# Moving weight and input loads, and cutting output tiles into half steps, in a fused attention and bilinear FFN kernel

## The chip, the cores and the metric

The kernel runs on one core of a Trainium2 chip. A core has five engines with instruction streams of their own: TensorE (PE, with its weight loads shown as PEld), VectorE (DVE), ScalarE (ACT), GpSimd (POOL) and SyncE (SP), and sixteen DMA engines that serve all DMA queues. The metric is device time in microseconds (us) of one execution; lower is better. Loads that change the type from float32 to bfloat16 are issued here from GpSimd (queue q0 of the profile); output stores and DMA transposes are issued from SyncE (queue q1).

## The reference

There are 4 batches of 8 heads, 768 rows and 64 columns a head. Rows form 8 blocks of 96. A small 8x8 matrix per head (`sort_net`) is normalised five times over rows and columns, and mixes the blocks of k and v. Each block of q then attends to its mixed block alone. The result, turned to 3072 tokens of 512 columns, goes through a bilinear FFN.

```python
for _ in range(5):
    P = exp(P - max(P)); P = P / sum(P, -1); P = P / sum(P, -2)
k_sorted = einsum('bhij,bhjcd->bhicd', P, k_b)      # the same for v
scores = scale * matmul(q_b, k_sb^T)                # per block of 96 rows
attn = softmax(scores)
x = matmul(attn, v_sb)                              # 4*768 tokens x 512
out = ((x @ w_a) * (x @ w_b)) @ w_out               # 512 -> 1536 -> 512
```

## The kernel before

Heads are worked in pairs: four pairs a batch, sixteen in all, numbered 0 to 15; pairs 4 to 7 are batch 1, pairs 8 to 11 batch 2. A pair has three units of attention work. **M** (`M`, line 507) mixes k and v with the spread matrices `s_all` (`pair_mix`, matmuls of line 281, copied to kT and vT by ScalarE and VectorE), turns v by a DMA transpose from SyncE (`turn_v`), and prepares the next pair's q: a copy on GpSimd (`pair_q`, line 265, two buffers `qc`) and a DMA transpose (`turn_q`, line 271, tile `qTf`). **R** (`pair_scores`) makes the scores (line 301) and their exponentials on ScalarE. **O** (`pair_o`) makes the outputs (line 249), has VectorE take reciprocals and scale them (lines 253 and 255, tile `xp`), in two halves, and turns them into `xT` by a DMA transpose (line 321). The score, output and mix tiles of PSUM share two buffers (pool `psA`).

The FFN of a batch is a list of steps on TensorE. `ffn_ab(b, m, t)` makes block m (128 columns) of x@w_a and x@w_b for half t of the tokens, eight matmuls of line 336, copied by ScalarE (356) and multiplied by VectorE (357) into `hT`. The output of batch 0 is made by `ffn_out` (line 377), six tiles of twelve matmuls with w_out, each copied by ScalarE (even tiles) or VectorE (odd tiles) to `o_sb`, which has two buffers, and stored by two DMAs. Batches 1 to 3 use Strassen's products instead (`ffn_out_pair`, line 434), with sums of the quarters of w_out that VectorE makes during batch 1 (`weight_sums`); only the last token tiles of batch 3 use plain products.

The order of all five engines is that of the program, written by hand (line 533). `interleave` (line 523) puts the attention units of batch b+1 between the FFN steps of batch b: after each step it emits units until their number reaches a share of the steps done. For batch 0's second half the steps are twelve `ffn_ab` and six `ffn_out`; the parameter `outs` counts each `ffn_out` as two steps. The order of the units of a batch is M0 M1 R0 M2 R1 O0 M3 R2 O1 R3 O2 O3, with the pair's number within the batch.

GpSimd issues the loads in program order and runs ahead of TensorE as far as buffers and DMA tracking allow: in the trace each load's issue starts just after the landing of the load eight places before it. A pair's k, v and q are loaded by three DMAs (`load_pair`, line 100; six buffers of each). The FFN weights w_a and w_b are loaded in six chunks of 256 columns each (`load_ab`, line 110), w_out in three (`load_out`, line 115). GpSimd also makes parts of `s_all` (`spread`, line 157) and the q copies. Pair 8's load is issued in O of pair 6, pair 9's in O of pair 7, pair 10's and 11's in M of pairs 8 and 9.

SyncE takes its transposes and stores in program order too, so each waits for those before it.

Of the kernel before, what the change touches and what calls it, by code (L numbers as in the profile page):

```python
# [9 lines left out]
FP32 = mybir.dt.float32  # L10
BF16 = mybir.dt.bfloat16
# [11 lines left out]
def kernel(  # L23
# [11 lines left out]
    nc = tc.nc  # L35
    P = 128
    B, H, S, D = q.shape
# [3 lines left out]
    DMODEL = H * D  # L41
# [4 lines left out]
    NCH = S // P  # L46
    HP = H // 2
    NPAIR = B * HP
    KA = DMODEL // P
    KO = DFF // P  # L50
    KH = KO // 2
# [6 lines left out]
    V0 = 16  # L58
    W = NCH * D
    HW = S // 2  # L60
    WC = 256
    NBUF = 3
    PSUM = bass.MemoryType.PSUM
    ET = mybir.EngineType
# [1 line left out]
    const = ctx.enter_context(tc.tile_pool(name="const", bufs=1))  # L66
# [5 lines left out]
    outp = ctx.enter_context(tc.tile_pool(name="outp", bufs=1))  # L72
    psA = ctx.enter_context(tc.tile_pool(name="psA", bufs=2, space=PSUM))
    psF = ctx.enter_context(tc.tile_pool(name="psF", bufs=4, space=PSUM))
# [18 lines left out]
    def load_pair(g):  # L93
        base = 2 * g * S * D
        tiles = []
        for name, t in (("k2", k), ("v2", v), ("q2", q)):
            if g < HP and name == "q2":
                continue
            to = ld.tile([P, 2, W], BF16, tag=name, name=name)
            nc.gpsimd.dma_start(out=to, in_=_ap(t, base, [[W, P], [S * D, 2], [1, W]]))  # L100
            tiles.append(to)
        loaded[g] = tiles
# [3 lines left out]
    w_out_sb = const.tile([P, KO, DMODEL], BF16, name="w_out_sb")  # L106

    def load_ab(c):
        for w_ap, w_sb in ((moe_w_a, w_a_sb), (moe_w_b, w_b_sb)):
            nc.gpsimd.dma_start(  # L110
                out=w_sb[:, :, c * WC:(c + 1) * WC],
                in_=w_ap.rearrange("(kc p) n -> p kc n", p=P)[:, :, c * WC:(c + 1) * WC])

    def load_out(c):
        nc.gpsimd.dma_start(
            out=w_out_sb[:, c * 4:(c + 1) * 4, :],
            in_=moe_w_out.rearrange("(kc p) n -> p kc n", p=P)[:, c * 4:(c + 1) * 4, :])
# [12 lines left out]
    kTs = [const.tile([P, S + PAD], BF16, name=f"kT{n}") for n in range(NBUF)]  # L130
# [23 lines left out]
    p_col = const.tile([P, NB, BH], BF16, name="p_col")  # L154

    def spread(eng, src, h0, n, i0=0, ni=NB):
        eng.tensor_tensor(
            out=s_all[:, h0:h0 + n, i0:i0 + ni],
            in0=_ap(mask, 0, [[CG, P], [0, n], [0, ni], [1, CG]]),
            in1=_ap(src, i0 * BH + h0, [[NB * BH, P], [1, n], [BH, ni], [0, CG]]),  # L160
            op=ALU.mult)

    def copy(eng, out, in_):
        if eng == "act":
            nc.scalar.copy(out=out, in_=in_)  # L165
        else:
            nc.vector.tensor_copy(out=out, in_=in_)
# [92 lines left out]

    def pair_q(g):
        qc = qtp.tile([P, NCH, 2, D], BF16, tag="qc", name="qc", bufs=2)
        nc.gpsimd.tensor_copy(out=qc.rearrange("p c e d -> p e c d"),  # L265
                              in_=loaded[g][2].rearrange("p e (c d) -> p e c d", c=NCH))
        st[g, "qc"] = qc

    def turn_q(g):
        qT = qtp.tile([P, NCH, P], BF16, tag="qTf", name="qTf", bufs=3)  # L270
        nc.sync.dma_start_transpose(out=qT, in_=st[g, "qc"].rearrange("p c e d -> p (c e d)"))
        st[g, "qT"] = qT

    def pair_mix(g, what, engines):
        src2 = loaded[g][0 if what == "k" else 1]
        to = (kTs if what == "k" else vTs)[g % NBUF]
        pitch, whole = (BLK, S + PAD) if what == "k" else (P, NB * P)
        mix = psA.tile([P, 2, 512], FP32, tag="A", name="mix")
        for c in range(NCH):
            for e in range(2):  # L280
                nc.tensor.matmul(  # L281
                    mix[e * D:(e + 1) * D, c // 3, c % 3 * P:(c % 3 + 1) * P],
                    lhsT=src2[:, e, c * D:(c + 1) * D],
                    rhs=s_all[:, 2 * g + e], start=True, stop=True)
        for hf, eng in enumerate(engines):
            d1 = _ap(to, hf * 3 * CG, [[whole, P], [CG, 3], [pitch, NB], [1, CG]])
            s1 = _ap(mix, hf * 512, [[1024, P], [P, 3], [CG, NB], [1, CG]])
            copy(eng, d1, s1)
# [19 lines left out]

    def pair_o(g):
        xp = att.tile([BLK, NB, 2, D], BF16, tag="xp", name="xp")  # L310
        if g == 2 * HP - 2:
            load_pair(2 * HP)
        elif g == 2 * HP - 1:
            load_pair(2 * HP + 1)
            pair_q(2 * HP)
            turn_q(2 * HP)
        elif g >= 2 * HP and g + HP < NPAIR:
            load_pair(g + HP)
        for hf in range(2):
            one_o(eTs[g % NBUF], hf, vss[g % NBUF], hf * NBH, xp, NB)  # L320
        nc.sync.dma_start_transpose(
            out=xT_of(g // HP)[:, g % HP, :].rearrange("p (i t) -> p i t", i=NB),
            in_=xp.rearrange("p i e d -> p (i e d)"))

    hTs = {}
# [34 lines left out]
    def store(b, c, o):  # L362
        if b == 0:
            h, u = divmod(c, 3)
            for c2 in range(2):
                nc.sync.dma_start(
                    out=_ap(out, (h * PH * NCH + 2 * u + c2) * DMODEL,
                            [[NCH * DMODEL, PH], [1, DMODEL]]),
                    in_=o[c2 * PH:(c2 + 1) * PH])
        else:  # L370
            rows = out[b * S:(b + 1) * S, :].rearrange("(p c) n -> c p n", c=NCH)
            nc.sync.dma_start(out=rows[c], in_=o)

    def ffn_out(b, c):
        po = psF.tile([P, DMODEL], FP32, tag="F", name="po")
        for m in range(KO):
            nc.tensor.matmul(po, lhsT=hTs[b][:, m, c * P:(c + 1) * P], rhs=w_out_sb[:, m, :],  # L377
                             start=(m == 0), stop=(m == KO - 1))
        o_sb = outp.tile([P, DMODEL], FP32, tag="o2", name="o_sb", bufs=2)
        copy("act" if c % 2 == 0 else "dve", o_sb, po)  # L380
        store(b, c, o_sb)

    def ffn_out_cut(b, c, cut):
        rows = out[b * S:(b + 1) * S, :].rearrange("(p c) n -> c p n", c=NCH)[c]
# [120 lines left out]

    def units_full(b):
        def M(g):
            pair_mix(g, "k", ("act", "act"))
            pair_mix(g, "v", ("dve", "act"))
            turn_v(g)  # L510
            if g in (2 * HP, 2 * HP + 1):
                load_pair(g + 2)
            if g + 1 < NPAIR and g + 1 != 2 * HP:
                pair_q(g + 1)
                turn_q(g + 1)

        g0 = b * HP
        order = [("M", 0), ("M", 1), ("R", 0), ("M", 2), ("R", 1), ("O", 0), ("M", 3),
                 ("R", 2), ("O", 1), ("R", 3), ("O", 2), ("O", 3)]
        what = {"M": M, "R": pair_scores, "O": pair_o}  # L520
        return [lambda w=w, n=n: what[w](g0 + n) for w, n in order]

    def interleave(steps, units, spare, slow=0, outs=0):
        n, done, at = len(steps), 0, 0
        for s, step in enumerate(steps):
            step()
            at += 1 if s < n - outs else 2
            want = s + 1 if s < slow else -(-at * len(units) // (n + outs - spare))
            while done < min(want, len(units)):
                units[done]()  # L530
                done += 1

    with tc.manual_schedule(engines={ET.PE, ET.Pool, ET.SP, ET.Activation, ET.DVE}):
# [105 lines left out]
                    half_x(0, 3, "act")  # L639
                ab_mms(begun[n], w_sb, 0, m, 0, range(KA - 1))  # L640

        load_ab(4)
        load_ab(5)
        load_pair(4)
        spread(nc.gpsimd, p_col, 8, 8)
        load_pair(5)
        for c in range(3):
            load_out(c)
        load_pair(6)
        pair_q(HP)  # L650
        turn_q(HP)
        load_pair(7)
        for n in range(2, 4):
            spread(nc.gpsimd, p_col, n * 8, 8)

        steps = [lambda: ffn_ab(0, 0, 0, begun[0:2]), lambda: ffn_ab(0, 1, 0, begun[2:4]),
                 lambda: ffn_ab(0, 2, 0, begun[4:5])]
# [3 lines left out]
        def outs(b):  # L661
            last = [NCH // 2 - 1] if b == B - 1 else []
            us = [u for u in range(NCH // 2) if u not in last]
            steps = [part for u in us for part in ffn_out_pair(b, u)]
            return steps + [lambda c=c: ffn_out(b, c) for u in last for c in (u,)] + [
                lambda: ffn_out_cut(b, u + 3, 3 * P) for u in last]

        steps = [lambda m=m: ffn_ab(0, m, 1) for m in range(KO)]
        steps += [lambda c=c: ffn_out(0, c) for c in range(NCH)]
        interleave(steps, units_full(1), 6, outs=NCH)  # L670

        halves = [n for m in range(KH) for n in (m, m + KH)]
        for b in range(1, B):
            steps = [lambda m=m, t=t, b=b: ffn_ab(b, m, t) for m in halves for t in range(2)]
            if b == 1:
                for m in range(KH):
                    steps[4 * m + 2] = lambda m=m: (weight_sums(m), ffn_ab(1, m + KH, 0))
            steps += outs(b)
            interleave(steps, units_full(b + 1) if b + 1 < B else [], 8, outs=0)


# [28 lines left out]
```

## Time and profile before

| | |
|---|---|
| median of 3 runs | 244.88 us (243.57, 244.88, 247.98) |
| the profiled execution | 245.97 us, its span 244.2 us |
| TensorE busy | 231.2 us |
| TensorE's clock | granted in full throughout |
| read from memory, written to it | 28.32 MB, 6.29 MB |
| loads by GpSimd's queue | 14.16 MB as written (bfloat16) |

Stages of the span, from the order of TensorE: up to 12 us normalisation and warming matmuls; 12 to 46 us attention of batch 0 and the first half of its FFN; 46 to 67 us the second half, with attention of batch 1 between; 67 to 86 us batch 0's output tiles, with the rest of batch 1's attention; from 86 us batches 1, 2 and 3, some 54 us for each of the first two and 49 for the last.

How to read it. Busy time is that of an engine's instructions; a matmul's end is modelled, so a busy TensorE is not one at its peak. A line of the order of an engine has start, duration, engine, line of the kernel, operation, tiles written and read, shape, count, and in brackets the idle time before it with what ended it. A line of the waits has who waited, for whom, the total in us, how often, and the longest. A line of "q" after an engine's name (SPq) is its sequencer, which issues DMAs; the time of such a line is that of the issue, and the landing is told apart. The row "DMA" of the page is the mean busy share of the DMA engines in 40 equal slices of 6.1 us, in tenths.

### The profile page before, as it was taken

Reading aid. Unit: us, or ns where it says so; the run is one execution under the profiler, and the core shown is the slowest. Engines: PE = TensorE matmul, PEld = TensorE weight load, DVE = VectorE, ACT = ScalarE, POOL = GpSimd, SP = SyncE. Lnnn points to the kernel's source line nnn. Section 1 sums busy time; section 2 is a strip of 40 time slices with the busy share of each in tenths; the row PEclk is TensorE's granted clock in tenths of the full one; section 3 lists DMA queues with packets and bytes.
Section 4 is the critical chain, followed back from the end, with each engine's and each line's share of the span. In section 5 each row is a group of like instructions: output and inputs, shape, how many; then the busy total and the mean of one; then the engine's idle time right before and its main releaser. Section 6 shows DMA issues by size and latency. Waiting matters only on the chain.

```text
span 244.2 us, 5906 instructions
## 1 busy us (share of the span) xinstructions
PE 231.2 (95%) x2399; PEld 154.1 (63%) x2403; DVE 149.7 (61%) x345; ACT 111.2 (46%) x220; POOL 61.4 (25%) x82
## 2 busy tenths in 40 slices
PE   7699899998979999999999999999999999999994
PEld 7476566665645456566578866566678866565873
DVE  6675466542635244888999464676867655575650
ACT  3565764475640056465342447456443333333321
POOL 8676767814344014092010001000000000000000
PEclk9999999999999999999999999999999999999999
DMA  5999999999999979999922439063106420000024
GB/s 79 199 199 197 196 201 206 177 181 139 138 151 226 213 189 122 117 120 162 168 61 67 160 120 133 1 78 75 35 0 70 169 89 0 0 1 4 0 89 172
DMA packets 56588, 28.72 MB, mean 118 GB/s; under 512 B 33392, under 2 KB 53616, under 8 KB 56560
## 3 DMA queue, kind: packets, MB, share of 16 engines
q0 software_dynamic: 20944, 14.16, 41.9%
q1 hardware_dynamic: 35472, 14.11, 32.5%
q8 instruction: 19, 0.31, 0.6%
q14 instruction: 9, 0.07, 0.1%
q10 hardware_dynamic: 144, 0.07, 0.1%
HBM read 28.32 MB, written 6.29 MB: 142 GB/s over the span
## 4 chain that ended last, share of the span: by engine, by line
PE 76%; DMA 11%; DVE 8%; issue 2%; ACT 1%; SPq 1%; POOL 0%; DVEq 0%
PE pf L336 46%; PE po L434 13%; DMA qTf<-qc 4%; PE po L377 3%; DMA q_first<-in_q_dram 3%; PE mix L281 3%; DMA xT<-xp 2%; PE o_ps L249 2%; DMA out_dram<-o_sb 2%; PE sc L301 2%; PE mixh L199 2%; DVE xp L255 2%; DVE hT L357 1%; DVE hs L427 1%; PE po L388 1%
## 5 line engine op out<-in xcount | busy, mean ns | idle before, releaser
L357 DVE TENSOR_TENSOR hT<-a_sb,pf 128x384 bf16<-128x384 bf16 x95 | 51.8, 552 | 54.7 <-PE pf L336 30.3
L336 PE MATMUL pf<-xT,w_a_sb 128*128 128x384 bf16 x380 | 78.0, 326 | 0.3 <-DMA xT<-xp 0.2
L336 PE MATMUL pf<-xT,w_b_sb 128*128 128x384 bf16 x380 | 77.4, 326 | 0.5 <-DVE hT L357 0.5
L356 ACT CAST a_sb<-pf 128x384 bf16<-128x384 f32 x95 | 45.4, 480 | 53.1 <-PE pf L336 36.2
L336 PEld LDWEIGHTS <-w_b_sb 128*128 128x128 bf16 x384 | 37.5, 98 | 26.2 <-issue 1.7
L336 PEld LDWEIGHTS <-w_a_sb 128*128 128x128 bf16 x384 | 34.9, 98 | 21.8
L265 POOL COPY qc<-q 128x768 bf16<-128x768 bf16 x12 | 10.0, 834 | 76.5 <-DMA qTf<-qc 54.6
L434 PE MATMUL po<-w_sum,hT 128*128 128x256 bf16 x192 | 22.8, 273 | 0.0
L306 ACT ACTIVATE eT<-sc 96x768 bf16<-96x768 f32 x24 | 18.2, 806 | 5.9 <-PE sc L301 5.8
L434 PEld LDWEIGHTS <-hT 128*128 128x128 bf16 x192 | 18.6, 98 | 2.2
L377 PE MATMUL po<-w_out_sb,hT 128*128 128x512 bf16 x80 | 18.7, 379 | 0.2
L255 DVE TENSOR_TENSOR xp<-o_ps,rec 96x512 bf16<-96x512 f32 x24 | 16.5, 686 | 0.8
L434 PEld LDWEIGHTS <-hs 128*128 128x128 bf16 x144 | 13.9, 98 | 1.6
L451 ACT COPY s<-po 128x512 f32<-128x512 f32 x8 | 4.7, 585 | 22.1 <-PE po L434 16.2
L377 PEld LDWEIGHTS <-hT 128*128 128x128 bf16 x84 | 8.0, 98 | 9.0
L165 ACT CAST kT<-mix 128x384 bf16<-128x384 f32 x24 | 10.3, 482 | 6.9 <-PE mix L281 6.9
L249 PEld LDWEIGHTS <-eT 96*128 96x128 bf16 x256 | 10.3, 97 | 3.6 <-DVE xp L255 1.4
L100 POOL DMA_DIRECT2D v<-in_v_dram x16 | 11.6, 728 | 3.3 <-DMA q_first<-in_q_dram 1.6
L249 PE MATMUL o_ps<-vs,eT 96*128 96x65 bf16 x256 | 11.5, 193 | 0.8 <-DVE xp L255 0.8
L100 POOL DMA_DIRECT2D k<-in_k_dram x16 | 11.7, 729 | 1.2 <-DMA w_a_sb<-in_moe_w_a_dram 0.6
L434 PE MATMUL po<-w_out_sb,hs 128*128 128x256 bf16 x96 | 11.8, 273 | 0.0
L467 DVE TENSOR_TENSOR o<-s 128x512 f32<-128x512 f32 x8 | 5.5, 688 | 9.1 <-ACT s L453 9.1
(92 smaller groups left out, 239.5 us busy)
## 6 DMA issues: line engine op xcount, KB each, us to landing
out_dram<-o SPq DMA_DIRECT2D x16, 256.0 KB, 2.2
k<-in_k_dram POOLq DMA_DIRECT2D x16, 192.0 KB, 8.5
v<-in_v_dram POOLq DMA_DIRECT2D x16, 192.0 KB, 8.4
q<-in_q_dram POOLq DMA_DIRECT2D x12, 192.0 KB, 9.8
w_a_sb<-in_moe_w_a_dram POOLq DMA_DIRECT2D x6, 256.0 KB, 9.7
w_b_sb<-in_moe_w_b_dram POOLq DMA_DIRECT2D x6, 256.0 KB, 10.6
w_out_sb<-in_moe_w_out_dram POOLq DMA_DIRECT2D x3, 512.0 KB, 12.1
out_dram<-o_sb SPq DMA_DIRECT2D x12, 128.0 KB, 4.0
```

The costliest lines, as they stand in the source:

```text
L100: nc.gpsimd.dma_start(out=to, in_=_ap(t, base, [[W, P], [S * D, 2], [1, W]]))
L165: nc.scalar.copy(out=out, in_=in_)
L249: nc.tensor.matmul(o_ps[:, e, i * (D + 1):(i + 1) * (D + 1)], lhsT=eT[:, hf, e, i * BLK:i * BLK + P], rhs=vs[0:BLK, i0 + i, V0 - 1 + e * ( ...
L255: nc.vector.tensor_tensor(out=_ap(xp, i0 * 2 * D, [[nxp * 2 * D, BLK], [D, 2], [2 * D, NBH], [1, D]]), in0=_ap(o_ps, 1, [[1024, BLK], [511 ...
L265: nc.gpsimd.tensor_copy(out=qc.rearrange("p c e d -> p e c d"), in_=loaded[g][2].rearrange("p e (c d) -> p e c d", c=NCH))
L281: nc.tensor.matmul(mix[e * D:(e + 1) * D, c // 3, c % 3 * P:(c % 3 + 1) * P], lhsT=src2[:, e, c * D:(c + 1) * D], rhs=s_all[:, 2 * g + e], ...
L306: nc.scalar.activation(out=eT[:, hf, :, 0:HB], in_=sc[0:BLK, :, 0:HB], func=AF.Exp, scale=float(scale))
L336: nc.tensor.matmul(pf[:, 0:HW], lhsT=w_sb[:, kc, m * P:(m + 1) * P], rhs=x_cols(b, kc, t), start=(kc == 0), stop=(kc == KA - 1))
L356: nc.scalar.copy(out=a_sb, in_=pf[:, 0:HW])
L357: nc.vector.tensor_mul(out=hT[:, m, t * HW:(t + 1) * HW], in0=a_sb, in1=ab[1][:, 0:HW])
L377: nc.tensor.matmul(po, lhsT=hTs[b][:, m, c * P:(c + 1) * P], rhs=w_out_sb[:, m, :], start=(m == 0), stop=(m == KO - 1))
L434: nc.tensor.matmul(to, lhsT=lhs(m)[:, u * P:(u + 1) * P], rhs=rhs[:, m], start=(m == 0), stop=(m == KH - 1))
```

## The change

- `load_ab` takes columns from `AB = (0, 256, 512, 1024, 1536)`: two chunks of 256 columns and two of 512. The calls for chunks 4 and 5 go; chunks 2 and 3 are issued where they were.
- The three DMAs of w_out are issued behind the loads of pairs 4 to 7, where they were between those of pairs 5 and 6.
- The parts of `s_all` for batches 2 and 3 are made in M of pairs 5 and 6, where they were made behind pair 7's load.
- `hold` copies one element of a given tile on GpSimd into a one-element tile. Pairs 8's and 9's loads are issued in O of pairs 6 and 7 as before, but behind the unit's matmuls and transpose, and behind a hold on its `xp`. Pairs 10's and 11's loads are issued in M of pairs 8 and 9 behind a hold on the `kT` just mixed. Later loads have no hold.
- The DMA transpose of pair 8's q moves from O of pair 7 to the start of M of pair 8.
- `ffn_out` returns two parts of six matmuls each, which become steps of their own; the copy and the stores belong to the second. `outs` of `interleave` goes, so each part counts as one step.

```diff
-    WC = 256
+    AB = (0, 256, 512, 1024, 1536)
...
-                out=w_sb[:, :, c * WC:(c + 1) * WC],
-                in_=w_ap.rearrange("(kc p) n -> p kc n", p=P)[:, :, c * WC:(c + 1) * WC])
+                out=w_sb[:, :, AB[c]:AB[c + 1]],
+                in_=w_ap.rearrange("(kc p) n -> p kc n", p=P)[:, :, AB[c]:AB[c + 1]])
...
+    held = const.tile([1, 1], BF16, name="held")
+
+    def hold(of):
+        nc.gpsimd.tensor_copy(out=held, in_=of)
...
     def pair_o(g):
         xp = att.tile([BLK, NB, 2, D], BF16, tag="xp", name="xp")
-        if g == 2 * HP - 2:
-            load_pair(2 * HP)
-        elif g == 2 * HP - 1:
-            load_pair(2 * HP + 1)
-            pair_q(2 * HP)
-            turn_q(2 * HP)
-        elif g >= 2 * HP and g + HP < NPAIR:
-            load_pair(g + HP)
         for hf in range(2):
             one_o(eTs[g % NBUF], hf, vss[g % NBUF], hf * NBH, xp, NB)
         nc.sync.dma_start_transpose(
...
+        if g == 2 * HP - 2:
+            hold(xp[0:1, 0, 0, 0:1])
+            load_pair(2 * HP)
+        elif g == 2 * HP - 1:
+            hold(xp[0:1, 0, 0, 0:1])
+            load_pair(2 * HP + 1)
+            pair_q(2 * HP)
+        elif g >= 2 * HP and g + HP < NPAIR:
+            load_pair(g + HP)
...
     def ffn_out(b, c):
-        po = psF.tile([P, DMODEL], FP32, tag="F", name="po")
-        for m in range(KO):
-            nc.tensor.matmul(po, lhsT=hTs[b][:, m, c * P:(c + 1) * P], rhs=w_out_sb[:, m, :],
-                             start=(m == 0), stop=(m == KO - 1))
-        o_sb = outp.tile([P, DMODEL], FP32, tag="o2", name="o_sb", bufs=2)
-        copy("act" if c % 2 == 0 else "dve", o_sb, po)
-        store(b, c, o_sb)
+        v = {}
+
+        def mms(ms):
+            for m in ms:
+                nc.tensor.matmul(v["po"], lhsT=hTs[b][:, m, c * P:(c + 1) * P],
+                                 rhs=w_out_sb[:, m, :], start=(m == 0), stop=(m == KO - 1))
+
+        def part1():
+            v["po"] = psF.tile([P, DMODEL], FP32, tag="F", name="po")
+            mms(range(KH))
+
+        def part2():
+            mms(range(KH, KO))
+            o_sb = outp.tile([P, DMODEL], FP32, tag="o2", name="o_sb", bufs=2)
+            copy("act" if c % 2 == 0 else "dve", o_sb, v["po"])
+            store(b, c, o_sb)
+
+        return [part1, part2]
...
         def M(g):
+            if g == 2 * HP:
+                turn_q(g)
             pair_mix(g, "k", ("act", "act"))
             pair_mix(g, "v", ("dve", "act"))
             turn_v(g)
             if g in (2 * HP, 2 * HP + 1):
+                hold(kTs[g % NBUF][0:1, 0:1])
                 load_pair(g + 2)
+            if g in (HP + 1, HP + 2):
+                spread(nc.gpsimd, p_col, (g - HP + 1) * 8, 8)
...
-    def interleave(steps, units, spare, slow=0, outs=0):
-        n, done, at = len(steps), 0, 0
+    def interleave(steps, units, spare, slow=0):
+        n, done = len(steps), 0
         for s, step in enumerate(steps):
             step()
-            at += 1 if s < n - outs else 2
-            want = s + 1 if s < slow else -(-at * len(units) // (n + outs - spare))
+            want = s + 1 if s < slow else -(-(s + 1) * len(units) // (n - spare))
...
-        load_ab(4)
-        load_ab(5)
         load_pair(4)
         spread(nc.gpsimd, p_col, 8, 8)
         load_pair(5)
-        for c in range(3):
-            load_out(c)
         load_pair(6)
         pair_q(HP)
         turn_q(HP)
         load_pair(7)
-        for n in range(2, 4):
-            spread(nc.gpsimd, p_col, n * 8, 8)
+        for c in range(3):
+            load_out(c)
...
-        steps += [lambda c=c: ffn_out(0, c) for c in range(NCH)]
-        interleave(steps, units_full(1), 6, outs=NCH)
+        steps += [part for c in range(NCH) for part in ffn_out(0, c)]
+        interleave(steps, units_full(1), 6)
```

More of the change, by code (lines that the diff above doesn't have):

```diff
@@ L664, in outs @@
             steps = [part for u in us for part in ffn_out_pair(b, u)]
-            return steps + [lambda c=c: ffn_out(b, c) for u in last for c in (u,)] + [
+            return steps + [part for u in last for part in ffn_out(b, u)] + [
                 lambda: ffn_out_cut(b, u + 3, 3 * P) for u in last]
         steps = [lambda m=m: ffn_ab(0, m, 1) for m in range(KO)]
-        steps += [lambda c=c: ffn_out(0, c) for c in range(NCH)]
-        interleave(steps, units_full(1), 6, outs=NCH)
+        steps += [part for c in range(NCH) for part in ffn_out(0, c)]
+        interleave(steps, units_full(1), 6)
         halves = [n for m in range(KH) for n in (m, m + KH)]
@@ L678 @@
             steps += outs(b)
-            interleave(steps, units_full(b + 1) if b + 1 < B else [], 8, outs=0)
+            interleave(steps, units_full(b + 1) if b + 1 < B else [], 8)
 _INS = ['q', 'k', 'v', 'sort_net', 'moe_w_a', 'moe_w_b', 'moe_w_out']
```

## The prediction

> **What bounds the kernel now.** I read the page's first two parts first, then TensorE's waits, then the order of TensorE and of SyncE from 46 to 90 us.
>
> ```profile
> PE 231.2 (95%) x2399; PEld 154.1 (63%) x2403; DVE 149.7 (61%) x345; ACT 111.2 (46%) x220; POOL 61.4 (25%) x82
> ...
> PEclk9999999999999999999999999999999999999999
> DMA  5999999999999979999922439063106420000024
> ```
>
> TensorE is busy for 95% at full clock, and the change leaves its products as they are. So only idle time can be won: 244.2 - 231.2 = 13.0 us, most of it at the two ends. The DMA engines are full up to slice 20 (122 us). TensorE's waits name what the middle holds:
>
> ```profile
> PE sc L301 <- DVE xp L255: 1.3, 2, 0.8
> PE sc L301 <- DMA qTf<-qc: 1.2, 1, 1.2
> ...
> PE pf L336 <- DMA xT<-xp: 0.2, 1, 0.2
> ```
>
> Only these three lie between 46 and 90 us, where the change acts: 2.7 us. TensorE's order shows where:
>
> ```profile
> 58.26 0.52 PE L301 MATMUL sc<-qTf,kT 64*128 64x96 bf16 x16 [1.22 <-DMA qTf<-qc]
> ...
> 69.75 0.65 PE L249 MATMUL o_ps<-vs,eT 96*128 96x65 bf16 x16
> 71.18 0.34 PE L301 MATMUL sc<-qTf,kT 64*128 64x96 bf16 x8 [0.78 <-DVE xp L255]
> 72.01 0.34 PE L301 MATMUL sc<-qTf,kT 64*128 64x96 bf16 x8 [0.49 <-DVE xp L255]
> ...
> 87.11 0.32 PE L336 MATMUL pf<-xT,w_a_sb 128*128 128x384 bf16 x1 [0.22 <-DMA xT<-xp]
> ```
>
> The first is R of pair 5, late for its turned q. The next two are R of pair 7: it stands directly behind O of pair 5, and the two psA buffers come free only when VectorE has scaled O's halves. The last is batch 1's first product, waiting for pair 7's xT. SyncE's order shows how transposes fare beside loads:
>
> ```profile
> 49.22 3.13 SPq L271 DMA_TRANSPOSE qTf<-qc  x1
> 52.39 4.61 SPq L291 DMA_TRANSPOSE vs<-vT  x1
> ...
> 80.10 1.29 SPq L271 DMA_TRANSPOSE qTf<-qc  x1
> 81.49 3.12 SPq L321 DMA_TRANSPOSE xT<-xp  x1
> 84.71 4.98 SPq L366 DMA_DIRECT2D out_dram<-o_sb  x6
> 90.02 1.23 SPq L291 DMA_TRANSPOSE vs<-vT  x1
> 91.34 1.26 SPq L271 DMA_TRANSPOSE qTf<-qc  x1
> ```
>
> An issue of 1.2 us becomes 3 to 4.6 us while loads are in flight; by the view of this tile, the one issued at 49.22 lands 8.9 us later, the one at 91.34 only 2.8 us later.
>
> **Wider ab chunks.** Four of twelve weight DMAs go: 4 x 0.74 us on GpSimd, which here waits for landings (0.2 to 0.65 us before most issues), so its time costs nothing. On the DMA engines, 256 KB chunks land 1.34 us apart (19.98 to 26.68, five steps); w_out's first 512 KB, in rows twice as wide, lands 2.50 us after the load before it. Eight chunks at 1.34 = 10.7 us become four at 2.5 = 10.0 us. What lies behind may land 0.7 us earlier; bounds 0 and 0.7. [...] The price is lateness of a chunk's first columns. Behind the landing at 22.70, four chunks of 2.5 to 2.7 us land at about 25.3, 28.0, 30.6 and 33.3. TensorE reads column 512 at 30.7 (block 4) and column 1024 at 38.0 (block 8): 2.7 and 4.7 us to spare, cost 0.
>
> **w_out behind batch 1's loads.** Pairs 5 to 7 come forward by up to the 9.3 us (40.41 to 49.71) that w_out's three transfers take; w_out then lands near 57, where q of pair 7 lands now. Its first reader is at 67.2: 10 us to spare. All bytes stay ahead of R of pair 5, so the queue ends where it did, less the 0.7 us. Its transpose stands behind that of pair 4's v on SyncE, as before. So its 1.22 us of waiting becomes about 0.6; bounds 0 and 2.2 (another landing of 1 us later). [...]
>
> **The spreads.** Two of 2.0 us each move from 43.9 us to M of pairs 5 and 6, ahead of their q copies. GpSimd idles 4.3 us before each of those copies, waiting for a copy's buffer. Their first reader is M of pair 8 at 88. Cost 0; without that cover q of pair 6 would be ready 2 us later, and SyncE takes it only at 57.04 anyway.
>
> **Output tiles as half steps.** Batch 0's six tiles become twelve steps of six matmuls (1.3 us). The old count gave each tile two points of 18 and the new one gives each half one, so the same rule puts O of pair 5 between the halves of tile 0, R of pair 7 behind tile 0, O of pair 6 behind tile 1, and O of pair 7 between the halves of tile 2. R of pair 7 gets 1.3 us of products ahead of it: it wants its second buffer 1.6 us after O's end at 70.4, that is at 72.0, when it now gets it. Its wait of 1.27 us goes to 0. What is late next is O of pair 7: it now stands 2.6 us behind O of pair 6, and then 1.3. VectorE copies tile 1 first (75.09 to 75.78), then scales O's halves until 77.45; O of pair 7 would want the second buffer at 75.4 + 1.3 + 0.25 = 76.95. A new wait of 0.5 us; bounds 0 and 0.8. One more switch between kinds of product costs 0.1 (1.41 against 1.30 us for eight products behind M). xT of pair 7 goes out 1.3 us earlier and without the 1.3 us transpose ahead of it: the 0.22 us goes.
>
> **Loads held until the o stage or the mix.** Each hold is a one-element copy on GpSimd; the trace has none. Its bounds are a 0.10 us memset and a 0.83 us q copy, I take 0.2. It queues up the load behind it, then the q copies. Pair 8's load now starts at 59.04, with no need for it until 88. Held by O of pair 6, whose first half is scaled at 76.62, less 1.87 us won by then (0.6 + 1.27), it starts at 75.0: k, v, q at 75.0, 75.7, 76.4. Loads in the two nearest stretches took 5.9 to 6.6 us (three from 95.05) and 5.0 to 11.1 us (six from 59.04, with transposes): v lands between 81.8 and 82.8. M of pair 8 would come at 88.0 - 1.5 = 86.5. Pair 9's goes out from 77.1; at the slow row's 10.4 us its v lands at 88.3, M of pair 9 is due at 90.0. Pair 10's is held by M of pair 8's first k copy (88.6 now, 87.1 then): v at 95, needed at 98. Cost 0, but the spare time is 2 to 4 us where it was over 10.
>
> **Pair 8's q transpose** moves from ahead of pair 7's xT to M of pair 8, behind six output stores. The last tile's products end at 86.3 - 1.3 = 85.0, its copy (0.69) at 85.8, its two stores 1.1 us later: 86.9. If its buffer waits for an earlier store, as now, it is 89.7. With 2.8 to 7.4 us to landing (the transposes at 91.34 and 94.83) it lands between 89.7 and 97.1; R of pair 8 stands at 95.08 - 1.5 = 93.6. From the middles, 88.3 + 5.1 = 93.4, it just holds; I charge 0.2, bounds 0 and 3.5.
>
> **Sum.** -0.6 - 1.27 + 0.5 - 0.22 + 0.1 + 0.2 = -1.3 us. The profiled execution took 245.97 us (its span 244.2 and 1.8 around it), so 244.7 for its like. It lies 1.1 above the median of 244.88; from that, 243.6.
>
> **Rivals.**
> 1. The held loads free more than I count: R of pair 5 has its q in time, and O of pair 7 and R of pair 8 wait for nothing. Then -1.22 - 1.27 - 0.22 + 0.1 = -2.6 us, 242.3. For it speak landings of 2.8 us without loads; against it, that R of pair 5 lies ahead of every hold.
> 2. The loads only change whom they disturb: pairs 8 and 9 now travel from 75 to 88 with the last xT and six stores. Landing 2.5 us later than taken, pair 8's transpose makes R of pair 8 wait about 1.5 us more, and the gain is returned: 244.9. The xT issue that stood 3.1 us at 81.49 speaks for it; that this issue had a q transpose ahead of it speaks against.
> 3. Slower: M of pair 8 waits for its own load. With the 14 us that loads from 37 to 43 us took, v lands at 89.7, 3.2 us late; its q at 90.4 is copied at 91.3 and turned by 100, 3 us behind R as it then stands. 243.6 + 6.2 = about 250. It decides from about 11 us to landing on; those loads had up to eight ahead of them, these have five at most.
> 4. The hold does not hold: if the copy is released by older data, the loads go at 60 as now and all but the half steps is as before: -0.6 to -1.0, 244.1. The dependency is on the tile just written, which speaks against.
>
> **How the numbers follow.** Forecast 0.58, rivals in order 0.15, 0.14, 0.06 and 0.07. Runs of the one kernel lie from 243.57 to 247.98, so a change of about 2% (4.9 us) is what can be told from none. Only rival 3, or an odd median, reaches that. The range takes rivals 1, 2 and 4 with the runs' own scatter: 241.2 to 247.0.
>
> **What the next profile would show.** Right: R of pair 7 without a wait for xp; a short one before O of pair 7; pair 8's load near 75; transposes from 60 to 75 us landing in 3 to 5 us instead of 8 to 11; no wait of the first product for xT. Wrong: a wait of M of pair 8 or 9 for k or v, of R of pair 8 for qTf over 0.5 us, of an early product for weights near 30 us, or R of pair 5 waiting 2 us.

## The result, and the profile after

The changed kernel takes 252.68 us (median of 4 runs, 251.72 to 253.41) against 244.25 us before (4 runs): a ratio of 1.035, 95% interval 1.029 to 1.042. It is 8.4 us slower where 1.3 us less was forecast. The profiled execution took 253.37 us, its span is 251.6 us, 7.4 us above that of before. Here and in the table of the experiments the medians are over all runs, and the ratios leave out runs over 1.5% above the fastest of their kernel, so the two can differ by a few tenths of a per cent.

The page of the changed kernel, parts 1 and 2:

```profile
PE 233.8 (93%) x2403; PEld 154.7 (61%) x2403; DVE 149.8 (60%) x345; ACT 110.9 (44%) x220; POOL 59.9 (24%) x82
...
PEclk9999999999999999799999999999999999999999
DMA  6999999999438979989999529462214330000024
```

TensorE is busy for 93% instead of 95%, and the clock has a 7 in slice 17 (101 to 107 us). The DMA row falls to 4 and 3 in slices 11 and 12 (63 to 75 us), where the loads now hold off, and is high again later than before. The longest of TensorE's waits between 46 and 142 us (who waited, for whom, total in us, times, longest):

```profile
PE sc L306 <- DMA qTf<-qc: 6.5, 2, 4.1
PE pf L342 <- DMA xT<-xp: 1.2, 1, 1.2
PE o_ps L249 <- DVE xp L255: 0.8, 2, 0.4
```

The order of TensorE puts them in place (start, duration, in brackets the idle time before the line):

```profile
58.79 0.52 PE L306 MATMUL sc<-qTf,kT 64*128 64x96 bf16 x16 [2.37 <-DMA qTf<-qc]
...
70.87 0.72 PE L306 MATMUL sc<-qTf,kT 64*128 64x96 bf16 x16
...
76.73 0.42 PE L249 MATMUL o_ps<-vs,eT 96*128 96x65 bf16 x8 [0.41 <-DVE xp L255]
...
87.94 0.32 PE L342 MATMUL pf<-xT,w_a_sb 128*128 128x384 bf16 x1 [1.23 <-DMA xT<-xp]
...
100.71 0.52 PE L306 MATMUL sc<-qTf,kT 64*128 64x96 bf16 x16 [4.10 <-DMA qTf<-qc]
101.16 1.41 PE L342 MATMUL pf<-xT,w_a_sb 128*128 128x384 bf16 x4
102.37 1.49 PE L342 MATMUL pf<-xT,w_b_sb 128*128 128x384 bf16 x4
```

R of pair 7, at 70.87, waits for nothing, as forecast. R of pair 5 waits longer, the first product of batch 1 waits 1.23 us for xT instead of 0.22, and R of pair 8, at 100.71, waits 4.10 us where it did not wait at all. Behind it four products take 1.4 us in place of 0.8: the granted clock was 0.53 from 101.2 to 104.8 us. The same place before, without a wait and at full clock:

```profile
95.01 0.51 PE L301 MATMUL sc<-qTf,kT 64*128 64x96 bf16 x16
95.45 0.82 PE L336 MATMUL pf<-xT,w_a_sb 128*128 128x384 bf16 x4
```

The slower clock is not peculiar to the profiled execution: the mean granted clock of the four runs is 0.986 to 0.993 (3.4 us at half clock in 251.6 us make 0.993), where 23 of the 25 runs of the kernel before that were taken beside e1 have 0.998 or more. SyncE shows what was late:

```profile
76.71 4.25 SPq L318 DMA_TRANSPOSE xT<-xp  x2
81.05 11.28 SPq L372 DMA_DIRECT2D out_dram<-o_sb  x8
92.42 1.36 SPq L276 DMA_TRANSPOSE qTf<-qc  x1
```

The last eight stores stretch from 81.1 to 92.3 us, and pair 8's q transpose stands behind them. It lands 8.2 us after 92.42. The first four of the eight, those of tiles 2 and 3, show why (who waited for them, us, times; then the time to landing):

```profile
L372 SPq DMA_DIRECT2D out_dram<-o_sb x4: 588/626/703, 81.1 to 83.2; - x4
  ACT o_sb L165: 10.2, 1
  DVE o_sb L167: 8.5, 1
DMA to landing us min/median/max: 7.0/7.4/7.4
```

The copies of tiles 4 and 5 wait for these stores to land. GpSimd shows when the held loads went:

```profile
75.91 0.18 POOL L266 COPY held<-xp 1x1 bf16<-1x1 bf16 x1 [16.28 <-DVE xp L255]
76.40 0.76 POOL L100 DMA_DIRECT2D k<-in_k_dram  x1 [0.32 <-PE o_ps L249]
...
90.81 0.18 POOL L266 COPY held<-kT 1x1 bf16<-1x1 bf16 x1 [4.30 <-ACT kT L165]
91.33 0.73 POOL L100 DMA_DIRECT2D k<-in_k_dram  x1 [0.34 <-issue]
```

The span's 7.4 us, from the two orders of TensorE:

| place | change, us |
|---|---|
| start to the point where R of pair 5 is due (57.04 before, 56.42 after) | -0.6 |
| wait of R of pair 5, 1.22 to 2.37 | +1.15 |
| waits of R of pair 7, 0.78 and 0.49 to none | -1.27 |
| new wait of O of pair 7 | +0.4 |
| first product of batch 1, 0.22 to 1.23 | +1.0 |
| two waits for the copies of tiles 4 and 5 (0.26 and 0.23) | +0.5 |
| R of pair 8 | +4.1 |
| 3.4 us at half clock | +1.7 |
| sum (the rest is small switches) | +7.0 |

### The profile page after: what moved, and what is told of

It is laid out like the page before. It is cut to its first block, busy times and chain, and to the rows that moved or that the text cites. A ratio compares the mean times of both kernels' runs of the same rounds, so it can differ in the third digit from the quotient of the medians.

```text
span 251.6 us, 5915 instructions
## 1 busy us (share of the span) xinstructions
PE 233.8 (93%) x2403; PEld 154.7 (61%) x2403; DVE 149.8 (60%) x345; ACT 110.9 (44%) x220; POOL 59.9 (24%) x82
## 5 line engine op out<-in xcount | busy, mean ns | idle before, releaser
L342 PE MATMUL pf<-xT,w_a_sb 128*128 128x384 bf16 x380 | 79.1, 330 | 1.6 <-DMA xT<-xp 1.2
L270 POOL COPY qc<-q 128x768 bf16<-128x768 bf16 x12 | 10.7, 892 | 66.0 <-DMA qTf<-qc 49.5
L306 PE MATMUL sc<-qTf,kT 64*128 64x96 bf16 x192 | 6.7, 204 | 7.2 <-DMA qTf<-qc 6.5
L165 ACT COPY o_sb<-po 128x512 f32<-128x512 f32 x4 | 2.3, 586 | 22.1 <-PE po L385 11.9
## 6 DMA issues: line engine op xcount, KB each, us to landing
out_dram<-o SPq DMA_DIRECT2D x16, 256.0 KB, 2.2
w_out_sb<-in_moe_w_out_dram POOLq DMA_DIRECT2D x3, 512.0 KB, 13.4
```

Of the source, the lines that this page charges most:

```text
L306: nc.tensor.matmul(sc[:, e, i * BLK:(i + 1) * BLK], lhsT=kT[e * D:(e + 1) * D, blk * BLK:blk * BLK + P], rhs=qT[e * D:(e + 1) * D, :, blk ...
L342: nc.tensor.matmul(pf[:, 0:HW], lhsT=w_sb[:, kc, m * P:(m + 1) * P], rhs=x_cols(b, kc, t), start=(kc == 0), stop=(kc == KA - 1))
```

## The experiments

Theory S, formed from this: the loads of pairs 8 and 9, held until 76 us, share the DMA engines with the last two xT transposes and the stores. The stores of tiles 2 and 3 take 7.0 to 7.4 us to land, where stores without loads beside them take 2.3 to 2.5 (e6, below); they keep both `o_sb` buffers, tiles 4 and 5 are copied only at 89.3 and 90.3, and their stores push pair 8's q transpose to 92.4, into pair 10's load. Theory P, the rival: the transpose's new place behind the stores is enough by itself. Theory L concerns R of pair 5 alone: the new order of the first loads makes its q later. The kernel before was run again beside each set of experiments; its median was 244.30 to 244.35 us.

| kernel | us (median) | ratio to before, 95% |
|---|---|---|
| changed kernel | 252.68 | 1.035 [1.029, 1.042] |
| e1: without any hold | 244.14 | 0.998 [0.995, 1.001] |
| e4: q transpose back in O of pair 7 | 250.69 | 1.023 [1.015, 1.031] |
| e2: before, with half steps only | 244.52 | 0.999 [0.996, 1.002] |
| e3: before, with the load order only | 245.24 | 0.999 [0.995, 1.002] |
| e5: holds on xp only | 249.84 | 1.016 [1.009, 1.022] |
| e6: holds on kT only | 243.75 | 0.995 [0.991, 0.999] |
| e11: the same once more | 244.38 | 0.999 [0.996, 1.001] |
| e7: wait of pair 8 filled | 251.04 | 1.022 [1.015, 1.029] |
| e8: one hold at pair 4, for both loads | 247.17 | 1.009 [1.005, 1.013] |
| e9: xp holds two pairs earlier, kT holds kept | 243.20 | 0.997 [0.9944, 0.9997] |
| e10: four o_sb buffers | 246.88 | 1.007 [1.003, 1.011] |

**e1, no holds.**

```diff
         if g == 2 * HP - 2:
-            hold(xp[0:1, 0, 0, 0:1])
             load_pair(2 * HP)
         elif g == 2 * HP - 1:
-            hold(xp[0:1, 0, 0, 0:1])
             load_pair(2 * HP + 1)
...
             if g in (2 * HP, 2 * HP + 1):
-                hold(kTs[g % NBUF][0:1, 0:1])
```

> The changed kernel without its four holds; pair 8's q transpose stays in M of pair 8, behind the stores. Theory S (the held loads of pairs 8 and 9 slow the stores of tiles 2 and 3 from 2.4 to 7.4 us, these keep the two o_sb buffers, tiles 4 and 5 are stored late, and the transpose behind them is issued at 92.4 us into pair 10's load): the loads go out near 60 and 70 us again, the transpose lands by 94, R of pair 8 waits under 0.5 us and TensorE's clock stays full. The 4.1 us wait and the 1.7 us of halved clock go, and most of the 1.2 us wait for xT: about 245 to 246 us. Theory P (the transpose's place behind six stores is enough by itself): R of pair 8 still waits 2 us or more, 249 to 251 us.

The whole loss goes: 244.14 us. The order of SyncE without holds:

```profile
75.65 3.30 SPq L318 DMA_TRANSPOSE xT<-xp  x2
79.04 8.61 SPq L370 DMA_DIRECT2D out_dram<-o_sb  x8
87.75 1.28 SPq L276 DMA_TRANSPOSE qTf<-qc  x1
```

The transpose is in the same place in the program as in the changed kernel, behind the same stores. It is issued 4.7 us earlier (1.1 of them because this execution's TensorE is that far ahead at O of pair 7), lands 2.8 us later, and R of pair 8 does not wait. Theory P falls: the place alone does no harm. The wait for xT is gone too. What stays is a 1.2 us wait of R of pair 7, whose q transpose, beside the unheld loads, takes 11.2 us to land.

**e4, the transpose back in O of pair 7, behind xT.**

```diff
             load_pair(2 * HP + 1)
             pair_q(2 * HP)
+            turn_q(2 * HP)
...
         def M(g):
-            if g == 2 * HP:
-                turn_q(g)
             pair_mix(g, "k", ("act", "act"))
```

> The changed kernel with pair 8's q transpose alone put back into O of pair 7, there behind that pair's xT transpose; the holds stay. Theory P: the transpose goes ahead of the stores and R of pair 8 waits for nothing: about 246 us. Theory S: the transpose cannot start before the held load of q has landed and been copied (86.5 us in the changed kernel's trace), and on SyncE the stores of tiles 2 to 5 now queue behind it; TensorE waits for the output buffers of those tiles or for o_sb before R of pair 8, 1.5 to 4 us, in place of the 4.1: 248 to 253 us.

250.69 us. TensorE's waits:

```profile
PE sc L306 <- DMA qTf<-qc: 2.8, 1, 2.8
PE pf L343 <- DMA xT<-xp: 2.4, 1, 2.4
```

R of pair 8 no longer waits, but the 2.8 us are those of R of pair 9 (whose transpose lands 12.9 us after 92.94, beside the loads of pairs 10 and 11), again with 3.4 us of half clock behind it, and the wait for xT has doubled, to 2.4 us. Why xT is later here is not shown. Theory P (246 us) falls again. Theory S had the size right (248 to 253 us) and the place wrong: it named the output buffers ahead of R of pair 8, and the copies into them cost 0.3 us.

**e2, half steps alone.** The kernel before with the new `ffn_out` in two parts, and:

```diff
-        steps += [lambda c=c: ffn_out(0, c) for c in range(NCH)]
-        interleave(steps, units_full(1), 6, outs=NCH)
+        steps += [part for c in range(NCH) for part in ffn_out(0, c)]
+        interleave(steps, units_full(1), 6)
```

> The kernel before with the output tiles as half steps and nothing else. Prediction's terms: R of pair 7's wait of 1.27 us goes, 0.5 us new before O of pair 7, the 0.22 us wait for xT goes: 1 us faster, about 243.3 us. Rival: with the loads still at 59 to 77 us, pair 7's q (which lands at 69.9) and v (which lands at 75.0) are late for R and O that now stand 1.3 us earlier, and the gain is returned: 244 to 245.5 us.

Both waits of R of pair 7 are gone in its profile, O of pair 7 waits 0.41 us, and the first product of batch 1 waits 1.07 us for xT. The product stands ready at 85.22 us instead of 86.89, 1.7 us earlier, but xT, with the loads of pairs 10 and 11 under way until 84.6, lands at 86.24 instead of 87.07, only 0.8 earlier. The time does not differ from before: the rival is right in the sum, though the late transfer is xT and not pair 7's q.

**e3, load order alone.** The kernel before with the new `AB` and `load_ab`, and:

```diff
-        load_ab(4)
-        load_ab(5)
         load_pair(4)
         spread(nc.gpsimd, p_col, 8, 8)
         load_pair(5)
-        for c in range(3):
-            load_out(c)
         load_pair(6)
...
         load_pair(7)
-        for n in range(2, 4):
-            spread(nc.gpsimd, p_col, n * 8, 8)
+        for c in range(3):
+            load_out(c)
...
                 load_pair(g + 2)
+            if g in (HP + 1, HP + 2):
+                spread(nc.gpsimd, p_col, (g - HP + 1) * 8, 8)
```

> The kernel before with the wider chunks, w_out behind batch 1's loads and the two spreads moved; no holds, no half steps. In the changed kernel R of pair 5 waits 2.37 us for its q against 1.22. Theory L (the wider rows of w_out beside the transposes, or the new order, cause it): R of pair 5 waits 2 to 2.6 us here too, and the time is 245 to 246 us. Rival (the extra wait only mirrors that TensorE came to R of pair 5 0.6 us earlier in that execution, or comes from elsewhere): the wait is 1 to 1.8 us and the time is within 0.5 us of before.

R of pair 5 does not wait in its profile, which neither forecast had, nor does it in six others with this order (e1, e4, e6, e7, e8, e10). In the changed kernel it waits 2.37 us, in e5 and e11 2.0 (there the profiled execution is the longest of its runs), in e9 1.68. The program up to that point is the same in all but e3. The DMA engines did not move the same transfers at the same rate; from 36 to 46 us, the changed kernel first, then e1, then e10 (columns: stretch, length, then the engines' busy times, and at the end clock, DMA share and GB/s):

```profile
36.00:46.00 10.00, 10.00 (x108) 6.23 (x106) 6.32 (x15) 4.11 (x9) 8.23 (x10) 1.00 1.44 179
```

```profile
36.00:46.00 10.00, 9.99 (x104) 6.16 (x103) 6.32 (x16) 4.29 (x8) 8.43 (x11) 1.00 1.31 196
```

```profile
36.00:46.00 10.00, 9.99 (x108) 6.21 (x106) 6.32 (x15) 4.09 (x9) 8.07 (x10) 1.00 1.41 183
```

The rate was 179 GB/s where R of pair 5 waits 2.37 us and 196 where it waits for nothing. But e10 has no wait at 183, and e9 waits at 185, so the rate of this stretch alone does not decide. Theory L, as a wait in every execution, is refuted: the same program has it in some executions and not in others, and the +1.15 us in the table comes from one that has it. Why stays open, and also whether the new order makes such executions more frequent: four of e3's ten runs took 247.6 to 249.7 us, and one of the 25 of the kernel before beside them took over 247. The ratio of 0.999 does not speak to that; otherwise the new order alone gives no difference that can be told.

**e5 and e6, the two kinds of hold apart.** Theory S is cut in two here: theory X has the harm in the holds on xp, theory K in those on kT. In e5 the holds on kT are taken out, in e6 those on xp.

```diff
             if g in (2 * HP, 2 * HP + 1):
-                hold(kTs[g % NBUF][0:1, 0:1])
                 load_pair(g + 2)
```

```diff
         if g == 2 * HP - 2:
-            hold(xp[0:1, 0, 0, 0:1])
             load_pair(2 * HP)
         elif g == 2 * HP - 1:
-            hold(xp[0:1, 0, 0, 0:1])
             load_pair(2 * HP + 1)
```

> The changed kernel with the holds on xp (loads of pairs 8 and 9) but without the holds on kT: pair 10's load follows pair 8's q copy at about 86.5 us, pair 11's follows pair 9's. Theory X (the holds on xp do the harm: loads at 76 to 81 us slow the last xT and the stores, and the q transpose behind the stores is late): the 1.2 us wait for xT and the transpose's issue near 92 us stay, and R of pair 8 still waits 2 us or more; 249 to 252 us. Theory K (the harm is that loads 10 and 11, held by kT, are in flight with the transposes of pairs 8 and 9): pair 10's load is through by 92, R of pair 8 waits under 1 us: 246 to 247 us.

> The changed kernel with the holds on kT (loads of pairs 10 and 11) but without those on xp: loads 8 and 9 go at about 58 to 62 us, loads 10 and 11 at 88 to 94. Theory X: stores and last xT are quick, the q transpose of pair 8 is issued before 88 and lands before R of pair 8; time as without any hold, 244 to 245 us. Theory K: the transposes of pairs 8 and 9 take 7 to 13 us beside loads 10 and 11, R of pair 8 or 9 waits 1 to 4 us, with or without a halved clock: 246 to 250 us.

With the holds on xp alone the kernel is 1.6% slower, with those on kT alone it is as fast as before or a shade faster (0.995 in one set of runs, 0.999 in the other). Both times fit theory X (249 to 252 us and 244 to 245) and not theory K. The one trace of e5 is that of the longest of its four runs (254.35 us): pair 8's transpose is issued there at 95.78, behind stores that stretch over 13.4 us, R of pair 8 waits 1.72 us, and the first product of batch 1 waits 3.24 us for xT. SyncE in e6:

```profile
75.21 3.45 SPq L318 DMA_TRANSPOSE xT<-xp  x2
78.75 7.83 SPq L370 DMA_DIRECT2D out_dram<-o_sb  x8
86.68 1.28 SPq L276 DMA_TRANSPOSE qTf<-qc  x1
```

The landings of the first four of these stores:

```profile
DMA to landing us min/median/max: 2.3/2.4/2.5
```

No load is in flight from 71 to 87 us, and the transpose lands in 2.9 us. It is the holds on xp that do the harm. The holds on kT add to it only together with them: pair 10's load, issued from 91.33, then meets a transpose that is late already, and it takes 8.2 us to land in the changed kernel. At the 2.8 us that a transpose takes without loads it would have landed at 95.2, before R of pair 8 stands ready at 96.6 (an estimate from these rows; e8 below shows such a case).

> The changed kernel with the holds on kT alone once more, beside the one above on the same chip: 243.3 to 244.2 us, a ratio to before of 0.991 to 0.999.

**e10, four o_sb buffers.** All holds in place.

```diff
-            o_sb = outp.tile([P, DMODEL], FP32, tag="o2", name="o_sb", bufs=2)
+            o_sb = outp.tile([P, DMODEL], FP32, tag="o2" if c % 4 < 2 else "o3", name="o_sb", bufs=2)
```

> The changed kernel, all holds in place, with four o_sb buffers in place of two (two of each of two kinds). If the chain runs over the buffers (slow stores of tiles 2 and 3 keep them, so tiles 4 and 5 are copied at 89 to 90 us and the q transpose of pair 8 is issued at 92.4), the transpose is issued at 86 to 88, before pair 10's load, and R of pair 8 waits under 1 us: 246.5 to 248.5 us, the 1.2 us for xT remaining. If the transpose is late by the loads in flight alone, or by its q copy, R of pair 8 still waits 2.5 us or more: 250 to 252.5 us.

246.88 us: 5.8 us less than the changed kernel, by two buffers. SyncE, then R of pair 8 on TensorE:

```profile
77.50 8.51 SPq L372 DMA_DIRECT2D out_dram<-o_sb  x8
86.15 1.24 SPq L276 DMA_TRANSPOSE qTf<-qc  x1
```

```profile
93.48 0.51 PE L306 MATMUL sc<-qTf,kT 64*128 64x96 bf16 x16
```

The stores are still slow beside the loads (5.2 to 8.7 us to landing), but nobody waits for them: SyncE reaches the transpose at 86.15, before pair 10's load (88.17), it lands 5.5 us later, R of pair 8 does not wait and the clock stays full. That is 6.3 us earlier than in the changed kernel's trace, of which 2.4 are its wait of R of pair 5; against e7 below, which like this execution has no such wait, it is 3.8. The 1.2 us for xT remain. With e1 and e6 this shows the chain: loads, stores, buffers, copies, stores, transpose, scores. The trace is that of the shortest of the four runs (244.31 us; the others took 246.8 to 248.2), so what holds the rest above the kernel before is seen in it only in part.

**e7, the wait filled.** Twenty matmuls of zeros, which no output uses, ahead of R of pair 8's scores.

```diff
+            if g == 2 * HP and hf == 0:
+                keep_busy(sc[:, 0], 20)
```

> The changed kernel with 20 matmuls of zeros, 512 columns each (4.3 us at full clock), ahead of R of pair 8's scores, to fill most of the wait of 4.1 us. If the halved clock of 3.4 us behind that wait comes from TensorE's idleness, the clock stays full and 1.7 us are won: about 251 us, span 250 or less for an execution like the one shown. If it comes from something else, the clock is halved there all the same and the time stays at 252.7 or grows by what the filling exceeds the wait.

```profile
94.15 4.48 PE L171 MATMUL sc<-warm 128*128 128x512 bf16 x20
98.56 0.52 PE L308 MATMUL sc<-qTf,kT 64*128 64x96 bf16 x16
99.01 0.82 PE L344 MATMUL pf<-xT,w_a_sb 128*128 128x384 bf16 x4
```

With TensorE busy through the wait, the products behind it take 0.8 us and the clock stays full. This is the shortest of four runs; one more has a mean clock of 1.000, the other two (252.5 and 256.0 us) have 0.993, and no trace tells where theirs was lost. The medians differ by 1.6 us, about what the half clock cost, but the runs scatter too widely to show it by time alone. So that idleness brings the half clock is supported here by one trace, not proved.

**e8 and e9, earlier holds.** e8 has one hold on the xp of pair 4 for both loads and none on kT. In e9 the holds on xp are those of pairs 4 and 5, and the holds on kT are kept. First e8's edit, then e9's:

```diff
-        if g == 2 * HP - 2:
+        if g == HP:
             hold(xp[0:1, 0, 0, 0:1])
             load_pair(2 * HP)
-        elif g == 2 * HP - 1:
-            hold(xp[0:1, 0, 0, 0:1])
             load_pair(2 * HP + 1)
+        elif g == 2 * HP - 1:
             pair_q(2 * HP)
...
             if g in (2 * HP, 2 * HP + 1):
-                hold(kTs[g % NBUF][0:1, 0:1])
                 load_pair(g + 2)
```

```diff
-        if g == 2 * HP - 2:
+        if g == HP:
             hold(xp[0:1, 0, 0, 0:1])
             load_pair(2 * HP)
-        elif g == 2 * HP - 1:
+        elif g == HP + 1:
             hold(xp[0:1, 0, 0, 0:1])
             load_pair(2 * HP + 1)
+        elif g == 2 * HP - 1:
             pair_q(2 * HP)
```

> The changed kernel with one hold alone: both loads of pairs 8 and 9 behind the first scaled half of O of pair 4 (about 60 us), none on kT. Without any hold the loads go at 57 us and pair 7's q transpose beside them takes 11 us, R of pair 7 waits 1.2 us. Theory X and K both: with the loads 3 to 5 us later the transpose of pair 7's q lands by 63, that wait goes, and the stores and pair 8's transpose stay as without holds: 1 to 1.5 us below the kernel without holds, 242.5 to 243.5 us. If instead any hold that pushes loads towards the stores costs, the time is 245 or more.

> The changed kernel with the holds on xp moved two pairs forward (pair 8's load behind O of pair 4, pair 9's behind O of pair 5), the holds on kT kept. Theory X (what matters is that no load is in flight from 74 to 87 us, with the last two xT and the stores): no wait for xT, none of R of pair 8, and R of pair 7 has its q by 63 us, so its wait of 1 us goes, too: 242.5 to 243.2 us, 0.5 to 1 us below the kernel with the holds on kT alone. If pair 9's load beside the transpose of pair 5's output costs as much as it did beside pair 7's, a wait of 1 us or more shows at O of pair 7 or at the first product of batch 1: 244 us or more.

e8 was a miss: 247.17 us, the case of its last sentence. Moving pair 8's and 9's loads later pushed the unheld loads of pairs 10 and 11 to 72 to 77 us, onto the same transposes and stores; xT took 9.9 us to land, and TensorE shows it, with half clock again behind a wait of 1.81 us:

```profile
86.66 0.32 PE L341 MATMUL pf<-xT,w_a_sb 128*128 128x384 bf16 x1 [1.81 <-DMA xT<-xp]
...
88.84 1.46 PE L341 MATMUL pf<-xT,w_a_sb 128*128 128x384 bf16 x4
```

So it does not matter whose loads these are. What matters is how late they still travel: loads were under way beside the last transposes of xT and the stores in the kernel before, too, but in e1 the last of them had landed by 82.7 us, there by 84.6, in e8 by 86.2 and in the changed kernel by 90.9. e8 shows one thing more. Its transpose of pair 8's q is issued almost as late as the changed kernel's, but lands 2.8 us later, with no load beside it, and R of pair 8 does not wait:

```profile
90.46 1.28 SPq L276 DMA_TRANSPOSE qTf<-qc  x1
```

In e9 pairs 8 and 9 go at 62 and 70 us and have landed by 79.6, pairs 10 and 11 go at 88 and 92. Pair 7's q lands 2.8 us after its issue instead of 11.2, R of pair 7 does not wait, nor the first product, nor R of pair 8. It takes 243.20 us against 244.33, 0.3% less with an interval that just leaves out 1. It has the lowest median found, but its interval overlaps those of e6 and e11, so a gain over the holds on kT alone is not shown. R of pair 5's 1.68 us are in its profiled execution.

## Why the prediction was wrong

The step that failed is "Loads held until the o stage or the mix", at "Cost 0". It asked only when the held data were needed, and there it was right: M of pairs 8 and 9 wait for no k or v. It did not ask what else travels while the held loads travel. Moving six transfers from about 60 to 76 us puts them beside the last two xT and the last eight stores, and the trace of before had the rows for it: with loads in flight the stores of tile 1 issued at 75.8 and 76.3 took over 5 us to land where those from 84.7 on took 2.3 to 2.7, and xT at 81.49 stood for 3.12 us. In place of 0 the step cost most of the 8.4 us: without any hold (e1) the time is that of before. In the traces these are 4.1 us at R of pair 8, 1.7 of half clock, 1.0 at the first product and 0.5 at the copies of tiles 4 and 5.

Point by point:

- **Pair 8's q transpose**, charged 0.2 us within 0 to 3.5, cost 4.1. The case was named, "If its buffer waits for an earlier store, as now, it is 89.7", and was judged by the old lateness. With loads beside the stores it became 92.4, and the landing 8.2 us instead of the middle value of 5.1. e10 shows that the wait for the buffer made it late, e8 that the lateness cost something only with pair 10's load beside the transpose.
- **The clock** was taken as full throughout, since every row of before had it so. Half clock behind the wait cost 1.7 us more; no term was made for it, and no row of before showed that there was one to make.
- **xT of pair 7**, "the 0.22 us goes": it became 1.23. It was issued 3 us earlier (78.4 instead of 81.5), but beside the held loads landed 9.5 us later instead of 5.6. e1, without the holds, has no such wait, so the step would have held with the loads elsewhere.
- **Half steps**: R of pair 7's 1.27 us went to 0 as worked out, and O of pair 7's new wait is 0.41 for 0.5 us forecast. By themselves (e2) they win nothing that can be measured, because the first product's wait for xT took their place: 1.07 us.
- **Wider chunks and w_out last**: no product waited for weights, as worked out. The chunks of 512 columns landed 2.5 to 2.8 us apart, as taken (256 KB in 1.34 us are 196 GB/s; 512 KB in 2.54 us are 206). The 0.6 us at R of pair 5 is no property of the program: of the eleven profiled executions with this order seven wait there for nothing and four for 1.7 to 2.4 us. In the kernel before, w_out's three transfers landed 2.5, 3.9 and 2.9 us after the load before each, and one transpose was in flight beside all three, from 40.27 to 50.28, so these rows do not show what a transpose costs beside them. The spreads cost nothing.
- **The hold itself** costs 0.18 us for the copy and about 0.3 us until the load's issue, not 0.2 in all; nothing depends on it.
- **Rivals.** Rival 2, "The loads only change whom they disturb", came nearest: it had the transfers that meet and the wait of R of pair 8, but priced at 1.5 us what came to 5.8 with the half clock, and it had neither the two `o_sb` buffers nor pair 10's load in it. Rival 3 had the sign and not the mechanism: loads landed in 5.5 to 10.7 us, not 14; that its time of about 250 us is near the measured one is luck. Rival 4 did not happen.
- **The sign of being right that came true**: transposes issued from 59 to 72 us landed in 2.8 to 3.5 us, as the profile was to show. In the kernel before TensorE waited for none of them; with the half steps and without holds R of pair 7 does, 1.2 us (e1), so that much was won.

## What to carry to other kernels

When a transfer is held back because nobody needs it yet, list what will travel beside it at its new time, stores and their buffers included, and follow each buffer to the instruction queued behind it. A store that takes 5 us longer costs nothing by itself (e10), but it can reach TensorE once its buffer is one of two and a transpose that scores need stands behind the next store. A wait of TensorE should be priced with the half clock that can follow it, 1.7 us here.

## What the runs showed of the hardware that was not expected

- Waits of TensorE of 1.81 us (e8), 2.02 (e11, R of pair 5), 2.81 (e4) and 4.10 (changed kernel) were each followed by 3.4 us at half clock: in the changed kernel 0.50 was granted from 101.25 to 104.67 us, and the mean granted clock of each of the four executions is 0.993. Waits of 2.37 us (changed kernel, R of pair 5) and 2.38 us (e4, xT) were not: four products behind each of them took 0.8 us. So the length of a wait alone doesn't decide; what does is not shown.
- In the same stretch of the same program (36 to 46 us) the DMA engines moved 178 GB/s in one execution (e11) and 196 in another (e1).
- One `w_sum` subtraction of VectorE took 0.91 us instead of 0.285 in the changed kernel, at 93 to 95 us, while GpSimd's q copy beside it (93.47) took 0.98 instead of 0.83.
